# Loading q and k of a windowed attention by GpSimd's casting transfers, with one group of heads worked by token halves and the hand-written order made anew

## The chip, the cores and the metric

The kernel runs on one core of a Trainium2 chip, as one launch. The metric is device time in microseconds (us), the median of several executions. Five engines have queues of their own: PE (TensorE, matrix products), DVE (VectorE), ACT (ScalarE), POOL (GpSimd) and SP (SyncE, which only issues transfers here). A profile of one execution gives the start and the length of every instruction, what it waited for, and the transfers.

## The reference, cut to what matters

```python
B, H, S, D = 8, 8, 576, 64
scores = (1 / sqrt(D)) * q @ k.T                 # per batch and head
mask = (rel >= 0) & (rel < 64)                   # rel = query position - key position
attn = softmax(where(mask, scores, -1e9))
x = (attn @ v) -> [B, S, H * D]                  # 576 tokens x 512

h = relu(x @ w_in)                               # 512 -> 1024
u, v = h[..., :512], h[..., 512:]
v_n = (v - mean(v)) / sqrt(var(v) + 1e-6)        # over the 512 features
v_s = einsum('ts,bsd->btd', w_spatial, v_n) + b_spatial
out = (u * v_s) @ w_out                          # [8, 576, 512], f32
```

All inputs are f32 in memory. The kernel computes in f16 with f32 accumulation.

## The kernel before

The work of a batch falls into steps, each with a name such as `S3_0`: kind S, batch 3, group 0 of the heads (heads 0 to 3; group 1 is heads 4 to 7). The attention steps of a batch and a group are these.

- `ldq`, `ldk`: load q and k of four heads as 128 rows of 1152 numbers. `tq`, `tk` (line 405, DVE): transpose them into `qkT` tiles.
- `ldv`: load V in five chunks of tokens. `hv` holds V in f16, `hs` the same shifted by 64 rows, filled by the copies `sl`, `su` and `s4`.
- `S` (line 494, PE): scores of the band into two pairs of PSUM banks. Step `E` (line 501, ACT): exponential. `M` (line 504, DVE): a minimum with a mask that holds 0 or a large number, which cuts the band. `Z` (line 517, PE): row sums by a matmul with ones. `N` and `n` (lines 544 and 546, ACT): the inverse by Ln and Exp. `P` (line 529, PE): the product with V. `X` (line 537, DVE): the scaling, into the f16 tile `x`. One `E`, `M`, `Z`, `P` and `X` serves two heads with all of the first 512 tokens; the names end in 0 and 1 for the two halves of the group's heads. The last 64 tokens of a batch, or of two batches, go through steps of their own with an `r` in the name (`S0_r`, `X0_r`).

The gating network of a batch has these steps, in 128-token groups `j` or 128-feature groups `i` (4 whole ones and a smaller fifth).

- `V` (x times the second half of w_in, PE), `Vr` (relu, line 684, ACT), `Vb`, `Va` (mean and variance, lines 686 and 688, DVE), `L1`, `L2` (one over the deviation, lines 731 and 733, ACT), `A` (normalise, line 743, DVE).
- `U` (first half of w_in times x, PE), `Ur` (relu, line 778, ACT), `G` (v_n times w_spatial, PE), `Ge` (gating, line 812, DVE), `O` (times w_out, PE), `Oe` (eviction, lines 662 and 850), `st` (store).

A group of V, U or O is four matmuls of 512 columns, a group of G five. The matmuls are issued in `halves` (lines 629 and 632): a step that the order marks `PH` is issued as pairs of 64-column halves. The spatial weights are transposed on PE (`W`, line 361) and copied out (`We`). `D` steps (line 877) are matmuls on zeros whose results nobody reads; they occupy PE at the start.

**Loads.** q and k of batches 0 to 2, V of batches 0 and 1 and all weights come by POOL's queue, whose transfers cast f32 to f16 on the way (lines 330, 344, 384, 422, 436). q and k of batches 3 to 7 come in f32 by SP's queue into eight `nat` buffers (line 395) and are cast by `cq` and `ck` into four `hqk` buffers; on POOL such a cast is three instructions of 384 columns (line 278). V of batches 2 to 7 comes in f32 by SP's queue into four `natv` buffers (line 448) and is cast by `cv`. A one-element copy on POOL, `hold` (line 393), keeps SP's first transfer back until the last early q has landed.

**The order.** The string `ORDER` (lines 18 to 140) lists every step with its engine and the buffers that it takes. `as_listed` (line 178) emits the steps in that order, so each engine and each queue works through its own steps as listed, and waits where something that a step needs isn't there yet. Nothing is reordered at run time.

Of the code, these are the lines that a sentence can't say: the load of q or k, first for batches 0 to 2, then for the others.

```python
c = add(f"ld{name}{b}_{g}", ("POOL", 0.55), key, lambda e: nc.gpsimd.dma_start(
    h.t.bitcast(f16)[:, 0:1152], src[b, 4 * g:4 * g + 4, :, :].rearrange("h (i j) d -> (h i) (j d)", j=18)),
    acq=[h])
...
ld = add(f"ld{name}{b}_{g}", ("DQ", 0.45), key, lambda e: nc.sync.dma_start(
    n.t[:, :], src[b, 4 * g:4 * g + 4, :, :].rearrange("h (i j) d -> (h i) (j d)", j=18)),
    deps=[hold], acq=[] if hold else [n], uses=[n] if hold else [], nbytes=1.57, n=128)
h = buf("hqk", f"h{name}{b}_{g}")
c = add(f"c{name}{b}_{g}", cost(1152), key,
        lambda e: cp(e, h.t[:, :], n.t[:, :]), deps=[ld], acq=[h], uses=[n])
```

Of the kernel before, what the change touches and what calls it, by code (L numbers as in the profile page):

```python
# [18 lines left out]
ldq0_0:POOL:0 ldk0_0:POOL:1 ldk0_1:POOL:2 keep:POOL ldv0_00:POOL:0 D24:PE:0 mask:DVE ldq0_1:POOL:3  # L19
D5:PE:1 ldv0_10:POOL:1 ldv0_01:POOL D21:PE:2 tq0_0:DVE:0 ldk1_0:POOL:4 D18:PE:3 D2:PE:0 D14:PE:1  # L20
D19:PE:2 D10:PE:3 ldv0_14:POOL ldv0_11:POOL D3:PE:0 D1:PE:1 D22:PE:2 D15:PE:3 tk0_0:DVE:1
S0_0:PE:0:1 tk0_1:DVE:2 E0_01:ACT:0 sl0_00:ACT:0 D6:PE:0 D0:PE:1 E0_00:ACT:1 su0_00:ACT D26:PE:2
ldv0_04:POOL M0_01:DVE Z0_01:PE:3 D23:PE:0 D8:PE:1 tq0_1:DVE:3 D16:PE:2 ldq1_0:POOL:5 S0_r:PE:1:0
E0_r0:ACT:0 D7:PE:0 E0_r1:ACT N0_01:ACT:0 M0_00:DVE Z0_00:PE:1 N0_00:ACT:1 ldwin1:POOL M0_r:DVE
Z0_r:PE:2 S0_1:PE:1:0 N0_r:ACT:2 D4:PE:0 sl0_10:ACT:1 tk1_0:DVE:4 su0_10:DVE E0_10:ACT:2 M0_10:DVE
s40_1:DVE sl0_11:DVE D12:PE:3 s40_0:DVE n0_00:ACT D20:PE:1 E0_11:ACT:3 M0_11:DVE sl0_01:POOL
su0_01:POOL P0_00:PE:2 X0_00:DVE:0 D11:PE:0 Z0_10:PE:3 D25:PE:1 su0_11:ACT n0_r:ACT P0_r:PE:0
X0_r:DVE:0 N0_10:ACT:3 n0_10:ACT tq1_0:DVE:5 P0_10:PE:1 Z0_11:PE:3 P0_01:PE:2 N0_11:ACT:4
X0_10:DVE:1 n0_01:ACT X0_01:DVE D13:PE:0 n0_11:ACT S1_0:PE:1:0 E1_00:ACT:1 P0_11:PE:3 E1_01:ACT:2
V0_4:PE:0 Vr0_4:ACT:0 X0_11:DVE V0_0:PH:1 V0_2:PE:2 M1_00:DVE ldq1_1:POOL:6 ldk1_1:POOL:7 M1_01:DVE  # L30
tq1_1:DVE:6 tk1_1:DVE:7 ldwin0:POOL Vr0_0:ACT:1 Z1_01:PE:3 N1_01:ACT:5 V0_1:PH:0 n1_01:ACT
Vr0_1:ACT:2 Vb0_1:DVE:0 V0_3:PH:1 Vr0_3:ACT:3 Vb0_3:DVE:1 Z1_00:PE:3 S1_1:PE:1:0 ldv1_00:POOL:2
Vr0_2:ACT:4 ldwsp0:POOL:0 ldwsp4:POOL:0 Vb0_2:DVE:2 D9:PE:0 ldv1_01:POOL E1_10:ACT:0 U0_4:PE:1
ldq2_0:POOL:1 U0_0:PE:2 U0_3:PE:0 E1_11:ACT:3 S1_r:PE:1:0 Ur0_0:ACT:0 consts:POOL Ur0_3:ACT:1
Vb0_0:DVE:3 Va0_0:DVE Va0_2:DVE M1_10:DVE E1_r0:ACT:0 U0_1:PE:2 ldb:POOL ldk2_0:POOL:2 Vb0_4:DVE:4
Va0_4:DVE sl1_00:DVE:2 Va0_1:DVE E1_r1:ACT Va0_3:DVE M1_11:DVE L10:ACT:0 Ur0_4:ACT:2 ldv1_10:POOL:3
ldv1_11:POOL L20:ACT A0_2:DVE:0 A0_3:DVE:1 A0_4:DVE A0_1:DVE:2 M1_r:DVE Ur0_1:ACT:3 U0_2:PE:0
Ur0_2:ACT:4 N1_00:ACT:1 W2:PE:1 We2:ACT A0_0:DVE:3 W3:PE:2 We3:ACT D17:PE:0 W4:PE:3 We4:ACT
sl1_01:DVE W1:PE:0 W0:PE:1 su1_00:DVE We1:DVE We0:DVE su1_01:DVE Z1_r:PE:2 n1_00:ACT N1_r:ACT:2
Z1_11:PE:0 N1_11:ACT:3 Z1_10:PE:3 G0_4:PH:1 N1_10:ACT:0 tq2_0:DVE:8 P1_00:PE:2 X1_00:DVE:2  # L40
sl1_10:ACT:3 n1_10:ACT su1_10:ACT G0_1:PH:0 ldv1_14:POOL P1_01:PE:3 G0_0:PH:2 Ge0_4:DVE:0
ldv1_04:POOL ldq2_1:POOL:3 tk2_0:DVE:0 X1_01:DVE Ge0_1:DVE:1 G0_2:PH:1 Ge0_2:DVE:2 ldk2_1:POOL:4
ldwo:POOL su1_11:POOL sl1_11:ACT P1_10:PE:3 s41_1:POOL hold:POOL:5 X1_10:DVE:3 S2_0:PE:1:0
P1_11:PE:0 ldq3_0:DQ cq3_0:POOL:0 n1_11:ACT X1_11:DVE s41_0:ACT ldv2_00:DQ:0 ldv2_03:DQ ldk3_0:DQ:6
ldv2_02:DQ G0_3:PH:1 Ge0_3:DVE:3 P1_r:PE:3 ck3_0:POOL:1 ldv2_01:DQ n1_r:ACT E2_01:ACT:1
ldv2_10:DQ:1 ldv2_13:DQ ldv2_14:DQ ldv2_11:DQ X1_r:DVE:1 tq2_1:DVE:1 V1_3:PH:0 E2_00:ACT:2
M2_00:DVE V1_0:PH:1 Vr1_0:ACT:5 tk2_1:DVE:2 V1_1:PH:3 Vr1_1:ACT:6 Ge0_0:DVE:4 Vr1_3:ACT:7 V1_2:PH:1
Vr1_2:ACT:4 V1_4:PE:3 Vb1_2:DVE:5 Vr1_4:ACT:3 M2_01:DVE Va1_2:DVE Vb1_3:DVE:3 Vb1_4:DVE:2
S2_1:PE:0:1 E2_11:ACT:0 U1_4:PE:0 E2_10:ACT:3 Va1_3:DVE U1_2:PE:1 Vb1_1:DVE:4 Va1_4:DVE Ur1_2:ACT:5
O0_2:PE:2 Oe0_4:ACT:0 S2_r:PE:1:0 Oe0_2:ACT:0 E2_r0:ACT:0 E2_r1:ACT Ur1_4:ACT:2 O0_3:PH:1 Oe0_3:ACT  # L50
ldq3_1:DQ:7 Z2_01:PE:3 U1_1:PH:2 N2_01:ACT:4 ldv2_12:DQ M2_11:DVE Va1_1:DVE U1_3:PH:0 Vb1_0:DVE:0
Va1_0:DVE M2_10:DVE L11:ACT:1 Z2_10:PE:1 Ur1_3:ACT:3 L21:ACT N2_10:ACT:1 O0_0:PH:3 U1_0:PH:0
Z2_00:PE:1 Ur1_1:ACT:4 Oe0_0:ACT:1 ldq5_0:DQ:0 tk3_0:DVE:3 tq3_0:DVE:4 S3_0:PE:1:0 Z2_11:PE:2
O0_1:PH:3 Ur1_0:ACT:1 N2_00:ACT:5 N2_11:ACT:0 Oe0_1:ACT M2_r:DVE Z2_r:PE:0 A1_2:DVE:4 A1_0:DVE:5
A1_4:DVE A1_1:DVE:6 A1_3:DVE:7 cv2_10:DVE:0 cv2_00:POOL:1 sl2_00:DVE:0 su2_00:DVE sl2_10:DVE:1
s42_1:POOL ldv2_04:DQ s42_0:POOL su2_10:POOL G1_3:PH:1 Ge1_3:DVE:5 P2_00:PE:2 G1_4:PH:3 ldk4_0:DQ:1
N2_r:ACT:3 n2_r:ACT cq3_1:POOL:2 n2_00:ACT X2_00:DVE:0 Ge1_4:DVE:6 P2_01:PE:0 cq5_0:POOL:3
G1_2:PH:1 n2_01:ACT X2_01:DVE E3_01:ACT:2 n2_11:ACT n2_10:ACT ldk3_1:DQ:2 ck3_1:ACT:1 P2_10:PE:2
M3_01:DVE P2_11:PE:3 ldq4_0:DQ:3 ldk4_1:DQ:4 E3_00:ACT:1 G1_0:PH:0 X2_10:DVE:1 X2_11:DVE
Ge1_0:DVE:7 tq3_1:DVE:5 G1_1:PH:2 Ge1_1:DVE:8 V2_3:PH:3 Vr2_3:ACT:0 V2_1:PH:0 Vr2_1:ACT:2 V2_0:PH:3  # L60
Vr2_0:ACT:1 Z3_01:PE:2 N3_01:ACT:2 V2_2:PH:0 Vr2_2:ACT:4 M3_00:DVE tk3_1:DVE:6 Ge1_2:DVE:9
S3_1:PE:0:1 E3_11:ACT:3 P2_r:PE:3 Vb2_2:DVE:1 cq4_0:POOL:0 st0_1:DQ ck4_0:POOL:2 Z3_00:PE:2
N3_00:ACT:5 E3_10:ACT:0 U2_3:PH:1 st0_4:DQ X2_r:DVE:0 V2_4:PE:0 Vr2_4:ACT:5 Oe1_4:ACT:0 O1_0:PE:3
Oe1_0:ACT:0 ck4_1:POOL:1 Vb2_0:DVE:5 ldv3_10:DQ:2 ldv3_13:DQ ldv3_00:DQ:3 ldv3_01:DQ ldv4_00:DQ:1
ldv4_04:DQ ldv3_11:DQ ldv4_03:DQ ldv3_04:DQ ldv3_12:DQ st0_0:DQ ldv3_14:DQ ldv3_03:DQ st1_4:DQ
ldq4_1:DQ:5 U2_0:PE:2 M3_11:DVE Ur2_0:ACT:0 U2_1:PH:0 Ur2_1:ACT:3 Z3_11:PE:3 tk4_0:DVE:7
Vb2_1:DVE:3 Va2_1:DVE cv3_10:POOL:2 sl3_10:POOL:2 tk4_1:DVE:0 S3_r:PE:1:0 E3_r0:ACT:0 E3_r1:ACT
N3_11:ACT:4 Ur2_3:ACT:2 U2_2:PE:2 Ur2_2:ACT:1 s43_1:POOL Vb2_4:DVE:2 O1_1:PE:0 O1_2:PE:3
cq4_1:POOL:2 Va2_2:DVE O1_3:PE:1 Vb2_3:DVE:4 ldv4_01:DQ Va2_0:DVE tq4_0:DVE:1 S4_0:PE:1:0 Va2_3:DVE
Va2_4:DVE Oe1_1:ACT L12:ACT:0 L22:ACT n3_11:ACT M3_r:DVE M3_10:DVE ldv3_02:DQ ldk5_1:DQ:6  # L70
ldv4_02:DQ su3_10:DVE Z3_r:PE:2 U2_4:PH:0 Oe1_2:ACT:1 Oe1_3:ACT N3_r:ACT:1 Ur2_4:ACT:4 Z3_10:PE:3
P3_10:PE:1 N3_10:ACT:0 n3_r:ACT n3_10:ACT P3_11:PE:2 A2_3:DVE:0 A2_1:DVE:1 A2_2:DVE:2 A2_0:DVE:3
A2_4:DVE G2_0:PE:0 E4_01:ACT:0 G2_2:PE:3 tq4_1:DVE:2 cv3_00:DVE:3 sl3_00:POOL:3 Ge2_0:DVE:0
X3_10:DVE:2 X3_11:DVE E4_00:ACT:3 s43_0:DVE Ge2_2:DVE:1 su3_00:ACT G2_4:PE:0 n3_00:ACT n3_01:ACT
G2_3:PE:1 Ge2_4:DVE:2 S4_1:PE:0:1 cv4_00:POOL:1 Ge2_3:DVE:3 P3_r:PE:2 P3_00:PE:3 X3_r:DVE:1
X3_00:DVE:3 G2_1:PE:0 P3_01:PE:1 V3_4:PE:2 E4_11:ACT:1 E4_10:ACT:2 M4_00:DVE X3_01:DVE Oe2_4:ACT:0
Ge2_1:DVE:4 Vr3_4:ACT:3 M4_11:DVE sl4_00:POOL:0 su4_00:POOL Z4_00:PE:3 N4_00:ACT:3 ldk5_0:DQ:7
ck5_0:POOL:1 V3_3:PH:1 Vr3_3:ACT:6 V3_1:PH:0 Vr3_1:ACT:7 n4_00:ACT V3_2:PH:2 Vr3_2:ACT:0 M4_01:DVE
Vb3_3:DVE:0 M4_10:DVE ldv5_00:DQ:0 V3_0:PH:3 Vr3_0:ACT:2 ldv5_10:DQ:2 ldv5_14:DQ ldv5_12:DQ
ldq6_1:DQ:2 ldv4_10:DQ:3 st1_0:DQ tq5_0:DVE:8 Vb3_4:DVE:3 Va3_4:DVE Z4_01:PE:1 Z4_11:PE:0  # L80
N4_01:ACT:0 n4_01:ACT N4_11:ACT:4 U3_1:PH:2 U3_0:PH:3 Ur3_1:ACT:5 Ur3_0:ACT:0 O2_0:PH:1 Vb3_2:DVE:1
cq6_1:POOL:0 Vb3_1:DVE:5 ldv4_12:DQ ldv5_04:DQ ldq5_1:DQ:0 ldv5_13:DQ cq5_1:POOL:2 ck5_1:POOL:3
Z4_10:PE:0 N4_10:ACT:1 P4_00:PE:2 Vb3_0:DVE:4 Va3_2:DVE X4_00:DVE:0 Va3_3:DVE Va3_0:DVE s44_0:ACT
Va3_1:DVE L13:ACT:1 Oe2_0:ACT:0 U3_3:PH:3 st1_1:DQ Ur3_3:ACT:1 tk5_0:DVE:3 ldq6_0:DQ:3 L23:ACT
tk5_1:DVE:4 A3_2:DVE:4 A3_4:DVE A3_0:DVE:5 U3_4:PE:0 U3_2:PE:2 Ur3_2:ACT:4 O2_2:PE:1 S5_0:PE:1:0
Ur3_4:ACT:2 A3_1:DVE:6 P4_01:PE:3 X4_01:DVE A3_3:DVE:7 E5_01:ACT:3 tq5_1:DVE:5 ldv4_11:DQ
ldv5_11:DQ ldv4_14:DQ M5_01:DVE ldv4_13:DQ ldk7_1:DQ:1 ldv5_02:DQ O2_1:PH:2 Oe2_1:ACT Oe2_2:ACT:1
O2_3:PH:0 Oe2_3:ACT E5_00:ACT:0 G3_3:PH:3 Ge3_3:DVE:6 M5_00:DVE G3_1:PH:2 Ge3_1:DVE:5 cv4_10:POOL:0
st2_4:DQ Z5_01:PE:1 sl4_10:POOL:1 s44_1:POOL G3_2:PH:0 G3_0:PH:3 su4_10:POOL P4_10:PE:2 ldv5_01:DQ
ldv5_03:DQ cv5_00:ACT:2 n4_10:ACT Ge3_2:DVE:7 N5_01:ACT:5 n4_11:ACT sl5_00:DVE:2 su5_00:POOL  # L90
# [842 lines left out]
```

## Time and profile before

| | us |
|---|---|
| median of 3 runs | 195.82 (195.31 to 196.53) |
| the profiled execution | 195.76 |
| its span, first to last instruction | 194.1 |
| PE busy | 185.5 |
| DVE busy | 162.0 |
| ACT busy | 150.5 |
| POOL busy | 84.7 |

How to read the rows that follow. A row of the timeline has the start in us from the span's start, the length, the engine, the line of the code, the operation, and what it writes and reads; in brackets stand the idle time of the engine just before it and what ended that. PEld are weight loads, which overlap the matmuls. A row of the groups has the busy time and the mean in nanoseconds of one instruction. POOLq and SPq are the queues' own entries. Of a matmul the end is modelled, so that lengths of matmuls overlap; the spacing of their starts tells the pace.

### The profile page before, as it was taken

The numbers are of one execution on the slowest core, as the hardware profiler recorded it, in microseconds if no ns is written. First come the engines' busy times: TensorE is split into PE (matmuls) and PEld (weight loads), VectorE is DVE, ScalarE is ACT, GpSimd is POOL, SyncE is SP. The second block draws the span as 40 slices with busy tenths as digits, with TensorE's granted clock in tenths as the row PEclk, the third lists the DMA queues.
The fourth block names the chain that finished last, engine by engine and source line by source line (L and its number), as shares of the span: only waits on it lengthen the run. The fifth ranks groups of instructions, "written<-read, shape, count | busy, mean of one in ns | idle before, by whom it ended". The sixth has DMA issues, their size and how long they took to land.

```text
span 194.1 us, 7423 instructions
## 1 busy us (share of the span) xinstructions
PE 185.5 (96%) x3167; PEld 112.0 (58%) x3167; DVE 162.0 (83%) x310; ACT 150.5 (78%) x272; POOL 84.7 (44%) x151
## 2 busy tenths in 40 slices
...
GB/s 72 190 164 187 197 193 181 143 225 301 208 351 396 223 184 220 322 277 264 269 232 243 328 320 148 84 257 179 5 75 77 111 5 0 138 0 137 132 140 191
DMA packets 50257, 35.74 MB, mean 184 GB/s; under 512 B 39216, under 2 KB 41712, under 8 KB 50224
## 3 DMA queue, kind: packets, MB, share of 16 engines
...
q8 instruction: 24, 0.39, 0.8%
...
## 4 chain that ended last, share of the span: by engine, by line
PE 74%; DMA 10%; POOL 6%; DVE 5%; issue 3%; DVEq 0%; POOLq 0%
PE bank L632 46%; PE bank L629 13%; DMA wsp<-in_moe_w_spatial_dram 6%; PE bank L529 4%; PE pair L494 4%; PE bank L517 3%; DMA hq<-in_q_dram 3%; POOL hv L422 3%; PE bank L717 3%; DMA hv<-in_v_dram 1%; POOL hk L384 1%; DVE x L537 1%; PE bank L612 1%; POOL hq L384 1%; PE bank L720 1%
## 5 line engine op out<-in xcount | busy, mean ns | idle before, releaser
L501 ACT ACTIVATE e<-pair 128x1024 f16<-128x1024 f32 x32 | 32.0, 1026 | 9.7 <-PE pair L494 8.4
L632 PE MATMUL bank<-wspT,vn 128*64 128x512 f16 (+3 forms) x460 | 34.9, 299 | 0.3 <-DVE x L537 0.2
L662 ACT COPY ob<-bank 128x512 f32<-128x512 f32 (+1 forms) x38 | 22.0, 591 | 11.9 <-PE bank L632 8.0
L686 DVE BATCH_NORM_STATS2 st<-vs 128x6 f32<-128x512 f16 (+1 forms) x40 | 26.2, 672 | 5.6 <-ACT vs L684 5.5
L812 DVE TENSOR_TENSOR g<-bank,ru 128x512 f16<-128x512 f32 (+1 forms) x36 | 23.0, 653 | 8.0 <-PE bank L632 5.3
L684 ACT ACTIVATE vs<-bank 128x512 f16<-128x512 f32 (+1 forms) x40 | 22.9, 595 | 7.0 <-PE bank L632 5.3
L632 PE MATMUL bank<-win,x 128*64 128x512 f16 x224 | 28.0, 380 | 0.0
L632 PEld LDWEIGHTS <-vn 128*64 128x64 f16 (+1 forms) x460 | 19.5, 111 | 11.6 <-issue 0.7
L632 PE MATMUL bank<-wout,g 128*64 128x512 f16 (+1 forms) x208 | 24.9, 371 | 0.0
L778 ACT ACTIVATE ru<-bank 128x512 f32<-128x512 f32 (+1 forms) x38 | 21.5, 581 | 4.0 <-PE bank L629 2.0
L632 PE MATMUL bank<-x,win 128*64 128x512 f16 (+2 forms) x264 | 24.1, 318 | 0.0
L504 DVE TENSOR_TENSOR e<-e,mask 128x1024 f16<-128x1024 f16 x32 | 22.3, 701 | 1.0 <-ACT e L501 0.9
L278 POOL CAST hq<-nq 128x384 f16<-128x384 f32 x24 | 13.2, 589 | 21.1 <-DMA nq<-in_q_dram 21.1
L537 DVE TENSOR_TENSOR x<-bank,lz 128x512 f16<-128x512 f32 x32 | 21.4, 681 | 1.1 <-PE bank L529 0.3
L405 DVE STREAM_TRANSPOSE kT<-hk 128x576 f32<-128x576 f32 x16 | 19.7, 1242 | 1.6 <-DMA hk<-in_k_dram 1.6
L544 ACT ACTIVATE lz<-bank 128x512 f32<-128x512 f32 x32 | 18.8, 598 | 2.6 <-PE bank L517 2.5
L405 DVE STREAM_TRANSPOSE qT<-hq 128x576 f32<-128x576 f32 x16 | 19.9, 1244 | 0.2
L546 ACT ACTIVATE lz<-lz 128x512 f32<-128x512 f32 x32 | 19.8, 631 | 0.3
L632 PEld LDWEIGHTS <-x 128*64 128x64 f16 x224 | 14.6, 110 | 8.6 <-issue 0.3
L278 POOL CAST hk<-nk 128x384 f16<-128x384 f32 x27 | 14.7, 579 | 8.6 <-DVE st L686 2.7
L632 PEld LDWEIGHTS <-g 128*64 128x64 f16 x208 | 13.8, 110 | 6.7 <-issue 0.4
L632 PEld LDWEIGHTS <-win 128*64 128x64 f16 x264 | 13.1, 110 | 7.2 <-issue 0.9
...
## 6 DMA issues: line engine op xcount, KB each, us to landing
...
hq<-in_q_dram POOLq DMA_DIRECT2D x6, 288.0 KB, 5.4
hk<-in_k_dram POOLq DMA_DIRECT2D x6, 288.0 KB, 6.1
...
```

Of the source, the lines that this page charges most:

```text
L278: nc.gpsimd.tensor_copy(o[:, n:n + 384], i[:, n:n + 384])
L405: d = add(f"t{name}{b}_{g}", ("DVE", 1.09), key, lambda e: nc.vector.transpose(qt.t[:, :].rearrange("p (i j) -> p j i", j=18), (h.t[:, 0:5 ...
L501: ex = add(f"E{b}_{g}{u}", ("ACT", 0.91), key, lambda e, u=u: nc.scalar.activation(e2[u].t[:, :, :], sc[u].t[:, :, :], AF.Exp, bias=0.0, s ...
L504: mins.append(add(f"M{b}_{g}{u}", ("DVE", 0.65), key, lambda e, u=u: nc.vector.tensor_tensor(e2[u].t[:, :, :], e2[u].t[:, :, :], mask[:, : ...
L537: lambda e, u=u, ob=ob, lz=lz: nc.vector.tensor_tensor(x.t[:, u, :], ob.t[:, :], lz.t[:, :], ALU.mult),
L629: nc.tensor.matmul(o[:, :], w, x, start=start, stop=stop)
L632: nc.tensor.matmul(o[c:c + 64, :], w[:, c:c + 64], x, start=start, stop=stop)
L662: lambda e: (nc.vector.tensor_copy if last else nc.scalar.copy)(view(), m.t[rows, 0:n]),
L684: rl = add(f"Vr{b}_{j}", ("ACT", 0.49), key, lambda e: nc.scalar.activation(vs.t[0:jn, :], m.t[0:jn, :], AF.Relu), deps=[pv], acq=[vs], us ...
L686: s1 = add(f"Vb{b}_{j}", ("DVE", 0.6), key + 0.02, lambda e: nc.vector.bn_stats(st6.t[0:jn, 0:6], vs.t[0:jn, :]), deps=[rl], acq=[st6], us ...
L778: lambda e, m=m, ru=ru, n=n: nc.scalar.activation(ru.t[:, 0:n], m.t[:, 0:n], AF.Relu), deps=[pu], acq=[ru], uses=[m])))
L812: nc.vector.tensor_tensor(g.t[:, 0:n], m.t[:, 0:n], ru.t[:, 0:n], ALU.mult)
```

## The change

- q and k of all batches are loaded by POOL's casting transfers, straight into `hqk`, of which there are now twelve. The steps `cq` and `ck` of batches 3 to 7 are gone, and the `nat` buffers too. The spatial weights pass through a `natv` buffer.
- V of batches 2 to 7 stays on SP's queue in f32, with six `natv` buffers instead of four. `hold` now waits for the last early V load and stands on POOL before the first V transfer of SP.
- Group 1 of batch 0 is worked by token halves: a new function `by_token` has one E (in two instructions), M, Z, N, n, P and X for 256 tokens of all four heads instead of 512 tokens of two heads. V0_0 and V0_1 need the first half only, V0_2 and V0_3 both heads' second half.
- The filler is 11 steps of four matmuls with 256 columns and 28 steps of one with 512, where it was 25 steps of two with 512 and two of nine with 128.
- The whole order is new. At its start the k and q loads of both groups of batch 0 come first on POOL, then `consts`, V loads, and `keep`; the mask stands on DVE behind the fourth transpose. All filler stands ahead of the first V0 step. In the new order one `cv` runs on ACT and one on DVE, ten on POOL (before: two, three and seven). The last output group is O7_5, evicted on ACT.

```diff
+BYTOKEN = {(0, 1)}
-NWARM, NFILL, FILL = 27, 2, 9
-BUFS = {"nat": 8, "natv": 4, "hqk": 4, ...
+NWARM, NFILL, FILL = 39, 28, 1
+BUFS = {"natv": 6, "hqk": 12, ...
...
-            if b <= 2:
-                h = buf("nat", f"h{name}{b}_{g}")
...
             h = buf("hqk", f"h{name}{b}_{g}")
-            c = add(f"c{name}{b}_{g}", cost(1152), key,
-                    lambda e: cp(e, h.t[:, :], n.t[:, :]), deps=[ld], acq=[h], uses=[n])
+            c = add(f"ld{name}{b}_{g}", ("POOL", 0.55), key, lambda e: nc.gpsimd.dma_start(
+                h.t[:, :], src[b, 4 * g:4 * g + 4, :, :].rearrange("h (i j) d -> (h i) (j d)", j=18)),
+                acq=[h])
...
+            if (b, g) == (2, 0):
+                held = HELD[0]
+                lds.append(add("hold", [("POOL", 0.1), ("ACT", 0.1)], key, lambda e: cp(
+                    e, nv.t[0:1, 0, 0, 0:1], held.t[0:1, 4, 0, 0:1]), deps=[HELD[1]], acq=[nv], uses=[held]))
...
+    def by_token(b, g, key, s, sc, e2):
...
+        for t in (0, 1):
+            ts = slice(256 * t, 256 * t + 256)
+            et = e2[t]
...
+                    lambda e, u=u, et=et, ts=ts: nc.scalar.activation(
+                        et.t[:, u, :].rearrange("p (w q) -> p w q", w=2), sc[u].t[:, :, ts],
+                        AF.Exp, bias=0.0, scale=0.125),
...
+                    for u in (0, 1):
+                        for w in (0, 1):
+                            nc.tensor.matmul(zb.t[64 * w:64 * w + 64, 256 * u:256 * u + 256], ones[:, :],
+                                             et.t[:, u, 256 * w:256 * w + 256], start=True, stop=True)
...
-                     deps=[XD[b, r] for r in range(4)] + [WIN[1, r] for r in range(4)],
+                     deps=[XD[b, r] for r in range(4)
+                           if not ((b, r // 2) in BYTOKEN and j // 2 != r % 2)]
+                     + [WIN[1, r] for r in range(4)],
...
-            for c in range(2 if i < NWARM - NFILL else FILL):
-                n = 512 if i < NWARM - NFILL else 128
+            for c in range(4 if i < NWARM - NFILL else FILL):
+                n = 256 if i < NWARM - NFILL else 512
```

The new order at the places that matter below (step, engine, buffer):

```diff
+ldk0_0:POOL:0 tk0_0:DVE:0 D0:PE:0 D1:PE:1 D2:PE:2 D3:PE:3 ldq0_0:POOL:1 tq0_0:DVE:1 D4:PE:0 D5:PE:1
+D6:PE:2 D7:PE:3 ldk0_1:POOL:2 ldq0_1:POOL:3 consts:POOL ldv0_00:POOL:0 ldv0_04:POOL ldv0_01:POOL
+keep:POOL ldk1_0:POOL:4 D8:PE:0 S0_0:PE:0:1 E0_00:ACT:0 E0_01:ACT:1 tk0_1:DVE:2 tq0_1:DVE:3 D9:PE:1
+D10:PE:2 D11:PE:3 D12:PE:0 ldv0_10:POOL:1 ldq1_0:POOL:5 ldv0_14:POOL D13:PE:1 D14:PE:2 D15:PE:3
+D16:PE:0 D17:PE:1 S0_r:PE:0:1 E0_r0:ACT:0 mask:DVE M0_00:DVE sl0_00:DVE:0 sl0_01:DVE E0_r1:ACT
+su0_01:DVE M0_01:DVE D18:PE:2 D19:PE:3 M0_r:DVE D20:PE:0 D21:PE:1 ldv0_11:POOL ldwin1:POOL D22:PE:2
+S0_1:PE:0:1 ldk1_1:POOL:6 E0_11a:ACT:2 E0_10a:ACT:3 ldq1_1:POOL:7 D23:PE:3 ldwin0:POOL su0_00:ACT
...
+D24:PE:0 ... Z0_00:PE:3 N0_00:ACT:0 tk1_0:DVE:4 E0_10b:ACT ... M0_10:DVE ...
+M0_11:DVE ... tq1_0:DVE:5 sl0_10:DVE:1 ... X0_00:DVE:0 su0_11:DVE su0_10:DVE ...
+s40_1:DVE s40_0:DVE ... X0_01:DVE D38:PE:1 n0_11:ACT X0_10:DVE:1 X0_11:DVE ...
+V0_1:PH:1 V0_3:PE:2 Z1_01:PE:3 ... V0_2:PH:0 ... V0_4:PE:2 ... Z1_00:PE:1 ... V0_0:PH:0 ... S1_1:PE:1:0
...
+s42_1:POOL ... ldk3_1:POOL:3 ldq4_0:POOL:4 ... ldk4_1:POOL:5
...
+su4_00:POOL tq4_1:DVE:2 ... ldq5_1:POOL:11
...
+st7_40:DQ Oe7_3:ACT st7_3:DQ st7_41:ACT O7_1:PH:3 Oe7_1:ACT O7_5:PH:2 Oe7_5:ACT st7_5:ACT st7_1:DQ
```

313 lines of the change are left out of this document (169 added, 144 removed).

## The prediction, made before the changed kernel ran

> **What bounds the kernel now.** I read the page's busy table first, then the same sums by stage (busy time of each engine between two times), then the chain of waits.
>
> ```profile
> span 194.1 us, 7423 instructions
> ...
> PE 185.5 (96%) x3167; PEld 112.0 (58%) x3167; DVE 162.0 (83%) x310; ACT 150.5 (78%) x272; POOL 84.7 (44%) x151
> ```
> ```profile
> 21.70:36.20 14.50, 14.26 (x192) 7.39 (x188) 13.64 (x30) 13.58 (x27) 9.99 (x17) 1.00 1.45 174
> ...
> 43.00:190.00 147.00, 145.84 (x2476) 89.98 (x2470) 126.20 (x240) 117.97 (x215) 54.75 (x97) 1.00 0.65 189
> ```
> ```profile
> 18.41 11.90 DMA wsp<-in_moe_w_spatial_dram
> ...
> 109.59 0.55 issue
> ...
> 112.54 5.18 PE bank L632 x48
> ```
> The columns of the second fence are: length of the stretch, then busy time of PE, weight loads, DVE, ACT and POOL, granted clock, DMA share, GB/s. From 43.0 to 190.0 PE is busy 145.84 of 147.00 us, at a clock of 1.00: this long stretch is bound by TensorE, and the change takes no matmul of the computation away. In it 24 pairs of half-width matmuls take 5.18 us, 0.216 us a pair, so a group V, U or O of four pairs costs 0.86 us and a group G of five 1.08. What is left to win there is idle time: 147.00 - 145.84 = 1.16 us, of which the chain names one piece of 0.55 at 109.59. Busy time of PE near the start says little, since most of it there is filler of line 877. So two stretches can move the end: the start, until PE has dense work, and the last 4 us. DVE is the engine behind both start stretches: from 21.7 to 36.2 it is busy 13.64 of 14.50.
>
> **The start, now.** These are DVE's instructions, of the timeline (start, length, what):
>
> ```profile
> 3.86 0.18 DVE L306 COPY mask<-keep 128x64 f16<-128x64 f16 x1 [2.52 <-POOL keep L302]
> ...
> 5.58 1.25 DVE L405 STREAM_TRANSPOSE qT<-hq 128x576 f32<-128x576 f32 x1
> 6.99 1.26 DVE L405 STREAM_TRANSPOSE kT<-hk 128x576 f32<-128x576 f32 x1 [0.16 <-DMA hk<-in_k_dram]
> 8.69 1.26 DVE L405 STREAM_TRANSPOSE kT<-hk 128x576 f32<-128x576 f32 x1 [0.45 <-DMA hk<-in_k_dram]
> ...
> 10.92 1.26 DVE L405 STREAM_TRANSPOSE qT<-hq 128x576 f32<-128x576 f32 x1
> 12.02 0.68 DVE L504 TENSOR_TENSOR e<-e,mask 128x1024 f16<-128x1024 f16 x1
> 13.62 0.43 DVE L589 TENSOR_TENSOR er<-er,mask 128x512 f16<-128x512 f16 x1 [0.93 <-ACT er L578]
> ...
> 17.33 0.69 DVE L283 COPY hs<-hv 64x256 f16<-64x256 f16 x3
> ...
> 20.69 2.04 DVE L537 TENSOR_TENSOR x<-bank,lz 128x512 f16<-128x512 f32 x3
> ```
> and these PE's, where the spatial-weight groups G0 and the second batch's V1 begin:
>
> ```profile
> 23.59 0.39 PE L629 MATMUL bank<-win,x 128*128 128x512 f16 x1
> ...
> 35.27 0.30 PE L597 MATMUL bank<-er,ones 128*64 128x128 f16 x4
> 35.74 0.62 PE L517 MATMUL bank<-e,ones 128*64 128x512 f16 x4 [0.17 <-DVE wspT L283]
> 36.17 0.82 PE L632 MATMUL bank<-wspT,vn 128*64 128x64 f16 x40
> ...
> 43.00 0.39 PE L632 MATMUL bank<-win,x 128*64 128x512 f16 x2
> ```
> By 23.59, where the third V0 group begins, two are done (1.7 us), so dense work began in effect near 21.9. I use 43.00, the first V1, as the mark: what lies before it is the start.
>
> **The start, after.** The first four transfers on the POOL queue are now k, q, k, q of batch 0, without V between. Successive loads were taken up at 5.58, 6.99 and 8.69, so 1.41 and 1.70 us apart; the fourth should be there at 10.1 to 10.4, I take 10.2, against 10.92 now. Against that, the mask, hidden on DVE from 3.86 to 5.58 until now (1.72 us), moves behind the fourth transpose, because `keep` stands behind `consts` and five V transfers in POOL's order. It now lies on DVE's own path. DVE's list up to X0_10, the piece that frees V0_1: transpose 1.26, mask 1.72, M0_00 0.68, three copies 0.7, M0_01 0.68, M0_r 0.43, a transpose 1.26, M0_10 and M0_11 1.36, a transpose 1.26, one copy 0.23, X0_00 0.68, four copies 0.92, X0_01 and X0_10 1.36: 12.5 us, from 10.2 to 22.7. Successive DVE instructions overlap a little (10.92 + 1.26 is 12.18, yet the next starts at 12.02); at up to 0.1 for some ten of them the end is 21.7 to 22.7, I take 22.2. The token halves show here: V0_1 starts without X0_11, the last quarter, which adds 0.68. Other costs of the halves: four exponentials of half size in place of two whole ones on ACT, and four Z matmuls in place of two of twice the width, the same columns. Both lie beside the DVE list.
>
> From 22.2 PE has five V0 groups 4.3, two Z 0.43, S1_1 0.6, four U0 groups 3.46, U0_4 0.47, S1_r 0.23 and the five W transposes 2.3 (estimates: 0.216 a pair, and for S, Z and W the pace of their steps in this trace): 34.0. The filler D9 and D17, which stood among them, is now ahead of V0. The other road to G0 is DVE again:
>
> ```profile
> L686 DVE BATCH_NORM_STATS2 st<-vs 128x6 f32<-128x512 f16 x32 | 21.1, 675 | 1.7 <-ACT vs L684 1.6
> ...
> L743 DVE TENSOR_SCALAR vn<-vs,mv,ln 128x512 f16<-128x512 f16 x32 | 12.7, 436 | 1.6 <-ACT ln L733 1.5
> ...
> L733 ACT ACTIVATE ln<-ln 128x5 f32<-128x5 f32 x8 | 1.6, 205 | 0.2
> ```
> X0_11 0.68, two masks 1.36, X0_r 0.4, two transposes 2.5, five statistics 3.4, a mask 0.68, five aggregates 0.5, Ln and Exp on ACT 0.5, five normalisations 2.2, two wspT copies 0.8, less the same overlap of 1.0: 22.2 + 12.0 = 34.2. So G0 starts near 34.4. Now it starts at 36.17 with three Z steps done before it (35.27 to 36.17, about 0.5 of real work), so at 35.6 on equal terms: 1.2 us gained. The spatial weights, 11.90 us in the chain now, land about as before or 0.8 earlier (one V pair no longer stands ahead of them), so they do not decide. From G0 to V1 the work is the same. **Start: -1.2 us**, with bounds -2.2 (overlap full, fourth load at 10.1) and +0.5 (no overlap, fourth load as late as now).
>
> **The middle.** What goes and what comes:
>
> ```profile
> L278 POOL CAST hk<-nk 128x384 f16<-128x384 f32 x27 | 14.7, 579 | 8.6 <-DVE st L686 2.7 <-DVE x L537 2.3 <-DVE qT L405 1.8
> L278 POOL CAST hq<-nq 128x384 f16<-128x384 f32 x24 | 13.2, 589 | 21.1 <-DMA nq<-in_q_dram 21.1
> L275 ACT CAST hq<-nq 128x1152 f16<-128x1152 f32 x1 | 1.2, 1152 | 0.0
> L283 DVE CAST hq<-nq 128x1152 f16<-128x1152 f32 x1 | 0.7, 744 | 0.0
> L283 DVE CAST hv<-nv 128x1024 f16<-128x1024 f32 x3 | 2.0, 680 | 0.0
> ```
> ```profile
> L384 POOL DMA_DIRECT2D hq<-in_q_dram x6: 543/572/666, 1.3 to 34.0; - x6
> L278 POOL CAST hq<-nq x24: 497/502/1096, 46.1 to 133.8; 128x384 f16<-128x384 f32 x24
> ```
> Twenty casts go: 27.9 us on POOL, 0.7 on DVE, two of about 1.15 on ACT. In the new order one V cast stays on DVE instead of three (-1.4) and one on ACT instead of two (-1.0). Some copies move too, three away from DVE (-0.7). Twenty issues come to POOL, 20 x 0.57 = 11.4 us, and leave SP. POOL was 54.75 of 147 busy, so this is hidden under PE. DVE loses some 2.8 of 126.2 us and ACT 3 to 4 of 118. PE waits for these two in the middle, so I take two thirds of the 1.16 idle: **-0.8 us**, bounds +1.5 (the new order brings a few waits of its own, each like the 0.55) and -1.2, all idle gone; waits shorter than a matmul's own 0.38 us do not show as idle, so -2 is not excluded.
>
> [...]
>
> **The tail.** Now and after, the last eviction and its store set the end:
>
> ```profile
> 187.54 0.38 ACT L850 COPY ob<-bank 128x256 f32<-128x256 f32 x1
> 189.18 0.59 ACT L662 COPY ob<-bank 128x512 f32<-128x512 f32 x1 [0.28 <-PE bank L632]
> 189.41 0.61 PE L861 MATMUL bank<-wout,g 128*64 128x256 f16 x8
> 190.11 0.42 DVE L662 COPY ob<-bank 128x256 f32<-128x256 f32 x1
> ```
> Now 0.70 us pass from 189.41 to the last copy and 0.42 in it. After, O7_5 (0.43) comes last, its 0.38 copy stands on ACT behind O7_1's 0.59 copy. Counted from the last group's start that is 0.2 + 0.48 + 0.38 = 1.06 against 1.12: **-0.05**.
>
> **Sum.** -1.2 - 0.8 - 0.05 = -2.05. The profiled execution took 195.76 us around its 194.1 us span, 0.06 under the median of 195.82: 195.76 - 2.05 = **193.7 us**.
>
> **Rivals.** First, *the start gives nothing*: the mask on DVE's path eats the earlier q, the G0 mark stays at 35.6, and only the middle's 0.8 and some of a new wait's 0.55 remain: about 195.3. For it: 1.72 us of mask against 0.7 of earlier q. Second, *the middle gives more*: PE's short waits for DVE and ACT go as well, -2 there, 192.5, or 191.5 with a start at its good bound. For it: DVE is nearly full until about 110; against: idle is 1.16. Third, *slower: loads behind copies on POOL.* The q and k loads now stand in POOL's order with the V casts and copies, which wait for V:
>
> ```profile
> POOL hv L281 <- DMA nv<-in_v_dram: 7.0, 4, 4.5
> POOL hs L283 <- DMA nv<-in_v_dram: 5.2, 1, 5.2
> ```
> ```profile
> hq<-in_q_dram POOLq DMA_DIRECT2D x6, 288.0 KB, 5.4
> ```
> ldk3_1, ldq4_0 and ldk4_1 stand behind s42_1, ldq5_1 behind su4_00. Between ldq5_1 and its transpose stand nine PE groups, about 8 us. With a wait of 5.2, a landing of 5.4 and the transpose of 1.26 a load is 3.9 us late, and PE stands: 193.7 + 3.9 = 197.6. It decides when POOL reaches a load less than 6.7 us before its transpose's turn. Against: twelve buffers let POOL run ahead by two batches. [...]
>
> **Chances.** Forecast 0.45 (own range 192.6 to 194.8), start gives nothing 0.22, middle gives more 0.18, slower 0.15. A measurement here tells about 1% from no change, so faster means under 193.9. The forecast case lies under it for 0.28 of its 0.45; with the second rival faster is 0.46; same is 0.17 + 0.22 = 0.39; slower 0.15. The range runs from the second rival's 191.5 to 197.2, which takes in the start's and the middle's bad bounds together but for 0.6 (195.76 + 0.5 + 1.5 = 197.8) and leaves out the worse half of the third.
>
> **What would show it.** Right: V0's first group near 22.2, G0's first near 34.4, V1's first near 41.8; issues of q and k on POOL near 0.57 us; no cast of nq or nk; PE idle from V1 on below 1 us. Wrong: the mask ends after 13.7, a q or k transpose of batches 3 to 7 waits for its DMA, or POOL's issues are 1 us and more.

## The result and the profile after

| | before | after |
|---|---|---|
| median, us | 195.83 (195.31 to 196.53, 4 runs) | 198.84 (198.28 to 202.82, 4 runs) |
| the profiled execution, us | 195.76 | 199.15 |
| its span, us | 194.1 | 197.2 |
| PE, DVE, ACT, POOL busy, us | 185.5, 162.0, 150.5, 84.7 | 184.8, 159.4, 148.8, 77.7 |

The kernel became slower: the ratio of after to before is 1.0119, with a 95% interval of 1.0075 to 1.0163. (The execution of 202.82, at a mean clock of 0.981, is left out of the ratio.) The forecast was 193.7, its range ended at 197.2.

I read the profile after as I had read that of before, the long stretch first. These are the busy times by stretch, with the columns of the prediction (length, PE, weight loads, DVE, ACT, POOL, clock, DMA share, GB/s):

```profile
84.00:98.00 14.00, 13.94 (x251) 8.60 (x248) 13.36 (x26) 12.29 (x24) 10.54 (x18) 1.00 0.99 222
98.00:113.50 15.50, 14.10 (x260) 7.82 (x258) 11.25 (x19) 13.35 (x24) 2.77 (x5) 1.00 0.98 182
...
43.30:193.00 149.70, 144.81 (x2490) 87.93 (x2484) 123.92 (x233) 118.01 (x216) 45.70 (x76) 1.00 0.65 150
```

From the first V1 group to 193.0, PE is idle for 149.70 - 144.81 = 4.89 us; before it was 1.16. PE's timeline shows one place that makes most of it:

```profile
111.25 1.03 PE L685 MATMUL bank<-wout,g 128*64 128x512 f16 x8
115.90 0.62 PE L513 MATMUL bank<-e,ones 128*64 128x512 f16 x4 [3.62 <-DVE e L500]
```

The two Z steps of batch 5's second heads wait for a mask step of DVE. So DVE's timeline comes next:

```profile
109.20 0.29 DVE L282 CAST hs<-nv 64x256 f16<-64x256 f32 x1
113.54 0.69 DVE L282 CAST hv<-nv 128x1024 f16<-128x1024 f32 x1 [4.06 <-DMA nv<-in_v_dram]
114.15 0.68 DVE L642 TENSOR_TENSOR er<-er,mask 128x1024 f16<-128x1024 f16 x1
114.75 1.09 DVE L500 TENSOR_TENSOR e<-e,mask 128x1024 f16<-128x1024 f16 x1
```

The masks were not late by themselves. DVE stood 4.06 us in `cv5_10`, the cast of batch 5's second V, and `M5_r` and `M5_11` are behind it in DVE's list. What was late is V. The timelines of the two that issue transfers, SP and POOL:

```profile
98.04 0.38 SPq L730 DMA_DIRECT2D out_dram<-ob  x1
98.47 12.58 SPq L441 DMA_DIRECT2D nv<-in_v_dram  x9
```
```profile
95.89 1.40 POOL L280 CAST hv<-nv 128x512 f16<-128x512 f32 x2 [1.51 <-PE bank L682]
97.36 1.23 POOL L280 COPY hs<-hv 64x512 f16<-64x512 f16 x2
98.54 1.17 POOL L386 DMA_DIRECT2D hq<-in_q_dram  x2
99.69 1.08 POOL L386 DMA_DIRECT2D hk<-in_k_dram  x2
```

From 98.47 on SP issues nine pieces of V, the first of them (`ldv5_11`) needed by `cv5_10`, the last three of that V (`ldv5_14`, `_13`, `_12`) at places 6 to 8. At 98.54 to 100.2 POOL issues four casting loads, which had stood behind POOL's cast and copies of V and so leave together. The view of the transfers, cut to 102 to 108 us, shows what the DMA engines did then (packets, MB, share of the 16 engines; q0 is POOL's queue, q1 SP's), and the same view for the issues from 98.4 to 102.6 shows how long V took (KB each, median us to landing):

```profile
q0 software_dynamic: 506, 1.04, 92.8%
q1 hardware_dynamic: 500, 0.13, 15.0%
```
```profile
hq<-in_q_dram POOLq DMA_DIRECT2D x2, 288.0 KB, 6.5
hk<-in_k_dram POOLq DMA_DIRECT2D x2, 288.0 KB, 9.0
...
nv<-in_v_dram SPq DMA_DIRECT2D x3, 128.0 KB, 10.9
nv<-in_v_dram SPq DMA_DIRECT2D x2, 64.0 KB, 10.6
```

In these 6 us the two queues sent about as many packets, 500 and 506. SP's are nearly all rows of V; of POOL's, 1.04 MB makes some 450 rows of q or k, and the rest are writes of 4 B (the view counts 553 packets under 512 B, so 53 of POOL's). But a row of V has 256 B and one of q 2304 B, and POOL's packets held the engines for 92.8% of the time: by these shares some 0.20 us for a row of q and 0.03 for one of V. From 108 to 110, with POOL's four loads nearly through (31 packets), SP's queue moved 1709. A piece of V took 10.9 us where the median of all of SP's V loads is 4.8. And the DMA engines were full anyway: their share is 0.98 and 0.99 in the two stretches above.

Two theories for the stall, then. **A, the order**: SP's list issues the last pieces of this V behind four pieces of later batches. **B, the shared engines**: q and k have a queue of their own now and hold up V whatever SP's order is.

For the start, the marks are these rows of PE:

```profile
22.63 1.05 PE L685 MATMUL bank<-win,x 128*64 128x512 f16 x8
...
35.22 1.25 PE L682 MATMUL bank<-wspT,vn 128*128 128x512 f16 x5
...
43.30 1.04 PE L682 MATMUL bank<-win,x 128*128 128x512 f16 x4
```

V1's first group is at 43.30 in place of 43.00: the start gave nothing. **Theory C**: the mask, which now stands on DVE's path, ate the gain.

### The profile page after: what moved, and what is told of

Read it like the earlier page. It is cut to its first block, busy times and chain, and to the rows that moved or that the text cites. A ratio compares the mean times of both kernels' runs of the same rounds, so it can differ in the third digit from the quotient of the medians.

```text
span 197.2 us, 7410 instructions
## 1 busy us (share of the span) xinstructions
PE 184.8 (94%) x3188; PEld 111.2 (56%) x3188; DVE 159.4 (81%) x304; ACT 148.8 (75%) x271; POOL 77.7 (39%) x134
## 4 chain that ended last, share of the span: by engine, by line
PE 55%; DVE 22%; DMA 6%; ACT 5%; issue 5%; SPq 4%; POOL 1%; DVEq 0%; POOLq 0%
PE bank L685 35%; PE bank L682 7%; SPq L441 4%; DMA hq<-in_q_dram 4%; DVE e L500 3%; PE bank L772 3%; PE pair L487 3%; DVE st L739 3%; DVE kT L393 3%; DMA nv<-in_v_dram 2%; PE bank L525 2%; DVE g L867 2%; PE bank L513 2%; DVE x L533 2%; DVE qT L393 2%
## 5 line engine op out<-in xcount | busy, mean ns | idle before, releaser
L685 PE MATMUL bank<-wspT,vn 128*64 128x512 f16 (+3 forms) x550 | 41.8, 299 | 0.0
L497 ACT ACTIVATE e<-pair 128x1024 f16<-128x1024 f32 x30 | 29.8, 1021 | 9.1 <-PE pair L487 8.7
L280 POOL COPY hs<-hv 64x512 f16<-64x512 f16 (+1 forms) x36 | 22.7, 661 | 21.4 <-DVE hv L282 13.6
L685 PEld LDWEIGHTS <-vn 128*64 128x64 f16 (+1 forms) x550 | 23.1, 111 | 13.1 <-DVE vn L798 0.5
L280 POOL CAST hv<-nv 128x512 f16<-128x512 f32 x20 | 13.0, 671 | 38.1 <-DMA nv<-in_v_dram 21.2
L685 PE MATMUL bank<-win,x 128*64 128x512 f16 x216 | 26.7, 379 | 0.0
L685 PE MATMUL bank<-x,win 128*64 128x512 f16 (+1 forms) x216 | 21.8, 332 | 0.0
L533 DVE TENSOR_TENSOR x<-bank,lz 128x512 f16<-128x512 f32 x30 | 20.0, 681 | 0.7 <-PE bank L525 0.2
L798 DVE TENSOR_SCALAR vn<-vs,mv,ln 128x512 f16<-128x512 f16 (+1 forms) x40 | 15.5, 442 | 4.2 <-ACT ln L788 4.2
L685 PEld LDWEIGHTS <-g 128*64 128x64 f16 x200 | 12.1, 110 | 7.0 <-issue 0.3
```

Source lines behind the costliest of these rows:

```text
L280: nc.gpsimd.tensor_copy(o[:, lo:hi, :, :], i[:, lo:hi, :, :])
L497: ex = add(f"E{b}_{g}{u}", ("ACT", 0.91), key, lambda e, u=u: nc.scalar.activation(e2[u].t[:, :, :], sc[u].t[:, :, :], AF.Exp, bias=0.0, s ...
L533: lambda e, u=u, ob=ob, lz=lz: nc.vector.tensor_tensor(x.t[:, u, :], ob.t[:, :], lz.t[:, :], ALU.mult),
L685: nc.tensor.matmul(o[c:c + 64, :], w[:, c:c + 64], x, start=start, stop=stop)
```

## The experiments

**V of batch 5 first on SP.** Ratios here and below are to the kernel before, on the same chip. The kernel after was not run again there, so its own ratio, 1.0119, is what they stand against.

```diff
-ldv4_04:DQ ldv6_00:DQ:3 ldv7_10:DQ:4 ldv7_14:DQ ... ldv5_14:DQ ldv5_13:DQ ldv5_12:DQ s45_0:DVE cv5_10:DVE:3
+ldv5_14:DQ ldv5_13:DQ ldv5_12:DQ ldv4_04:DQ ldv6_00:DQ:3 ldv7_10:DQ:4 ldv7_14:DQ ... s45_0:DVE cv5_10:DVE:3
```

> The last three pieces of batch 5's second V (ldv5_14, ldv5_13, ldv5_12) are issued on SP's queue ahead of four pieces of batches 4, 6 and 7; nothing else moves. Theory A (the order on SP's queue): these pieces went out at 106.47 to 108.69, behind four others; now they go out by 101.5, land with the usual 5 us at about 106, the cast cv5_10 starts at its turn on DVE (109.5 against 113.54), the idle of PE of 3.62 us at 112 is gone and the time is 199.15 - 3.6 = 195.5. Theory B (the DMA engines are shared between two queues, and the four casting loads of q and k that POOL issues from 98.5 to 100.2 starve the small rows of V): the piece ahead of them, ldv5_11, went out at 98.47 already and landed at 110.53 only; it will land there again, the three behind it at 110.9 to 111.9, the cast starts near 111.9 and half the stall, 1.6 to 2.0 us, is left: about 197.4.

Measured: 194.87 us (193.06 to 198.21, 10 runs), ratio 0.990 (0.9855 to 0.9946). The stall is gone, PE is busy 13.00 of the 13 us from 98 to 111. That is A's number, but the trace shows more than A. Here the issues of V from 97.7 to 101.3, and, in a second fence, those from 101.8 to 103.5, just after POOL's first casting load at 101.83:

```profile
L441 SPq DMA_DIRECT2D nv<-in_v_dram x5: 505/607/1505, 97.8 to 101.2; - x5
...
DMA to landing us min/median/max: 2.7/2.8/4.0
```
```profile
L441 SPq DMA_DIRECT2D nv<-in_v_dram x3: 461/550/607, 101.9 to 103.1; - x3
...
DMA to landing us min/median/max: 6.1/10.3/10.4
```

V that went out before the casting loads took 2.8 us, V that went out after them 10.3. The repair moved the right pieces ahead of the casting loads, by 0.6 us. B's mechanism is there; its forecast failed because POOL came 3.3 us later here than in the profile after.

**Three casting loads behind V.**

```diff
-... Oe2_1:ACT ldq7_0:POOL:3 Z5_11:PE:2 ... ldk7_1:POOL:4 ldk6_1:POOL:5 ... sl5_10:POOL:3
+... Oe2_1:ACT sl5_10:POOL:3 ldq7_0:POOL:3 Z5_11:PE:2 ... ldk7_1:POOL:4 ldk6_1:POOL:5 ...
```

> POOL's copy sl5_10, which needs all of batch 5's second V, is put ahead of the three casting loads ldq7_0, ldk7_1 and ldk6_1, so these are issued only when that V has landed; SP's list is as before. Theory A (order on SP's queue): the last pieces still go out near 108.7 and land at 113, the stall stays, 199. Theory B (the casting loads starve V): with one casting load in place of four beside it, ldv5_11 lands by 105 in place of 110.53, SP's issues are no longer held up (one of them took 3.96 us), all four pieces are there by 108, the 3.62 us of idle are gone and the time is near 195.5, unless ldk6_1 now comes too late for its transpose.

Measured: 194.67 us (193.6 to 195.73), ratio 0.9904 (0.9859 to 0.995). SP's list is that of the kernel after, piece for piece, and the stall is gone. All eight pieces from 98.3 on:

```profile
L441 SPq DMA_DIRECT2D nv<-in_v_dram x8: 451/606/1140, 98.3 to 103.4; - x8
...
DMA to landing us min/median/max: 3.0/3.6/4.5
```

So A alone is refuted: the order on SP does no harm when the casting loads stay away. With the run before, either thing that parts the two takes the stall away.

**The cast of V on POOL.**

```diff
-... s45_0:DVE cv5_10:DVE:3 Ur4_0:ACT:3 ... sl5_10:POOL:3
+... s45_0:DVE Ur4_0:ACT:3 ... cv5_10:POOL:3 sl5_10:POOL:3
```

> The cast cv5_10 goes from DVE to POOL, just ahead of sl5_10; the order of all transfers is the same. Both theories leave the landing of V at 113.0 to 113.5. If the stall is made by DVE's order (the masks M5_r and M5_11 stand behind the waiting cast, Z5_11 and Z5_10 wait for the masks), these four run at once and PE goes on; POOL then needs two casts of 0.61, two copies of 0.6 and 0.4 and two of 0.61 after 113.5, so P5_10 finds its V at 117.2 where PE would be at 115.6: 1.6 us of idle at another place, total about 197.1. If the masks wait for something else, no change: 199.

Measured: 194.61 us (193.67 to 195.5), ratio 0.9913 (0.9874 to 0.9953). POOL's cast starts at 113.21 after 8.96 us of waiting for V, so V is as late as in the kernel after, and yet most of the stall is gone. What is left stands where expected, in two pieces of 0.88 and 0.24 us and short waits, about 1.5 in all:

```profile
115.55 0.22 PE L525 MATMUL bank<-e,hs 128*64 128x64 f16 x2 [0.88 <-POOL hs L280]
...
116.11 0.22 PE L525 MATMUL bank<-e,hs 128*64 128x64 f16 x2 [0.24 <-POOL hs L280]
```

That shows the last link: a late V cost 3.62 us because DVE, in order, held two masks behind it that had no need of V. The total fell 2.5 us further than the 197.1 that I expected; this was not traced in full.

**The loads alone.** This run and the next are one execution each. In the first the stages overlapped, so that its numbers are bounds only: V alone landed in 3.0 to 3.3 us, beside casting loads in 9.4 to 11.2.

> Loads alone, six stages one after the other, each of four pieces of V (128 KB, rows of 256 B) or four loads of q (128 rows) or both; nothing of the reference is computed, the output is zeros. From the kernel after: a casting row holds its DMA engine 218 ns, an f32 row 223 ns, a V row 20 ns; so four loads of q are 7 us of all 16 engines and four pieces of V 2.5 us. Stage a, V on SP alone: last piece lands 2.5 to 3.5 us after its issue. Stage b, four casting loads alone: the last lands about 7 us after the first begins to move. Stage c, four casting loads on POOL and V on SP issued at the same time. Theory B (rows of both queues take turns, each turn of q ten times as long): V lands with or after the last of q, 8 to 10 us after its issue. Theory A (the queues share by bytes or not at all): V lands within 5 us. Stage d, q as f32 and V behind it, both on SP: V lands after q, about 8 us. Stage e, q as f32 on ACT's queue and V on SP: as c if any two queues do it, within 5 us if it is a matter of the casting queue. Stage f, all on POOL, q first: as d.

The second run parts the stages by copies on DVE.

```diff
+    phases = [("a", nc.gpsimd, 0, 1), ("b", nc.gpsimd, 4, 0), ("c", nc.gpsimd, 1, 1), ("d", nc.gpsimd, 2, 1),
+              ("e", nc.gpsimd, 4, 1), ("f", nc.scalar, 4, 1), ("g", nc.sync, 4, 1), ("h", nc.sync, 4, 0),
+              ("i", nc.gpsimd, 4, 2)]       # queue of q, loads of q, V (2: ahead of q)
```

> The loads alone again, with stages that do not overlap: nothing of the reference is computed. In each stage four pieces of V (128 KB, rows of 256 B) go out on SP's queue, beside none, one, two or four casting loads of q on POOL issued at the same moment (stages a, c, d, e), beside four f32 loads of q on ACT's queue (f), behind four f32 loads on SP's own queue (g), and 1 us or more ahead of four casting loads (i); stage b is four casting loads alone, h four f32 loads alone. If rows of the two queues take turns and a row of q holds its engine ten times as long as one of V, the last V piece lands with the last load of q: about 3 us after its issue alone, then 5, 7 and 10 as one, two and four casting loads stand beside it, 8 to 10 in f as well, and 3 to 4 in i, where V has gone ahead. If it is a matter of the casting queue alone, f stays at 4. Casting buys no DMA time: b and h take the same from first to last landing, 1.5 to 1.8 us a load.

Measured, in the view of the transfers (median to landing of four pieces of V; the last letter is the stage):

```profile
va<-in_v_dram SPq DMA_DIRECT2D x4, 128.0 KB, 2.9
vc<-in_v_dram SPq DMA_DIRECT2D x4, 128.0 KB, 4.7
vd<-in_v_dram SPq DMA_DIRECT2D x4, 128.0 KB, 4.9
ve<-in_v_dram SPq DMA_DIRECT2D x4, 128.0 KB, 7.1
vf<-in_v_dram SPq DMA_DIRECT2D x4, 128.0 KB, 8.5
vg<-in_v_dram SPq DMA_DIRECT2D x4, 128.0 KB, 7.4
vi<-in_v_dram SPq DMA_DIRECT2D x4, 128.0 KB, 3.3
```

The slowest piece took 3.0 us alone (a), 4.9, 5.7 and 9.2 beside one, two and four casting loads (c, d, e). It is not a matter of casting: with q as f32 on ACT's queue (f) it was 8.6. Behind q on SP's own queue (g) it was 7.5: there V waits too, but a list for one queue says so. In stage i three pieces went ahead and took 2.2 to 3.7 us; the fourth was issued at 72.49, 0.3 us after the first casting load, and landed at 82.4.

The last rows of that piece went out beside rows of q. The view of the transfers from 81.5 to 82.0 gives the rate in 40 slices of 0.0125 us, and the packets of the two queues:

```profile
GB/s 0 205 0 184 0 0 0 0 0 0 0 0 0 0 0 184 0 20 0 184 0 0 0 0 0 0 0 0 0 0 0 0 0 20 0 0 0 0 0 0
...
q0 software_dynamic: 7, 0.01, 10.2%
q1 hardware_dynamic: 4, 0.00, 1.3%
```

In one slice a row of V is 20 GB/s, a row of q 184, and one of each 205. So a row of V started at 81.52, 81.72 and 81.92, 0.20 us apart, and a row of q takes 0.19 us in this trace (from 78.0 to 82.4 q0's 301 packets, 40 of them small, held the 16 engines for 72.4% of the time). It was much the same since 78.0: the view from there to 82.4 has 23 packets of q1, the piece's last 22 rows and one small write, and the rows came some 0.18 us apart. Each load or piece has 16 such small writes here (stage b: 576 packets for four loads of 128 rows; stage e: 2112 of q1 for four pieces of 512), so 15 of this one's were out before 78.0. That only one of the 16 engines was left with the 22 rows is my estimate from this; no view names the engine of a packet. The last row started at 81.92, the sixteenth write is the fourth packet of q1 above, and the piece was reported landed at 82.4.

The spacing fits queues that take turns row by row: one row of V in 0.20 us, beside a row of q of 0.19 us.

Casting bought no time of the DMA engines here: four casting loads alone (b) held them for 79.9% of 8.3 us, 6.6 us, four f32 loads (h) for 73.2% of 8.6, 6.3 us.

**The casting loads alone in the old order.** From the kernel before: q and k of batches 3 to 7 on POOL at the places that SP had, the casts gone, 16 `hqk` buffers and a fifth `natv` for the spatial weights.

```diff
-ldq3_0:DQ cq3_0:POOL:0 ... ldk3_0:DQ:6 ... ck3_0:POOL:1
+ldq3_0:POOL:12 ... ldk3_0:POOL:13 ...
```

> The kernel before with the first part of the change alone: q and k of batches 3 to 7 come by casting loads on POOL at the places in the list where SP had them, the twenty casts are gone (27.9 us of POOL's work), and everything else, the order, the mask, the halves by heads, is as before. Theory A (the new order made the stall, the queues are innocent): no slower than before, 194.5 to 195.8. Theory B (what makes V late is that q and k now have a queue of their own beside it): V pieces issued beside casting loads take 10 us and more here too, where the list was made for one queue; 197 to 200, with PE waiting for V or for a copy that waits for V.

Measured: 200.65 us, ratio 1.0233 (1.0164 to 1.0302). That looked like B, but two filler steps had come out too long, and V1 stood at 46.92. So once more, with the filler of the kernel before:

> As the kernel before with casting loads of q and k alone, but with the filler matmuls of the kernel before too: in the earlier run two filler steps had come out with 512 columns in place of 128 (2.99 against 1.54 us and 1.90 against 0.68), and V1's first group stood at 46.92 in place of 43.00 because of it, while from there to the last group 145.92 us passed against 145.97. If only the filler made that run slow: V1 near 43.0 to 44.0 and 195.5 to 197.0, which means that casting loads in the old order cost nothing by themselves and bring nothing, though POOL is freed of 27.9 us (Theory A). If sharing the DMA engines between two queues costs in this order too (Theory B), PE waits for V or its copies somewhere from V1 on: 198 and more.

Measured: 195.99 us (194.89 to 197.86, 10 runs), ratio 0.999 (0.9958 to 1.0023). By itself the first part of the change is worth nothing, though it takes 27.9 us of casts off POOL (whose busy time falls from 84.7 to 66.7). The profiled execution is a long one, 197.72 us, and it shows that the loads are not simply harmless. SP, in its timeline:

```profile
87.42 12.88 SPq L443 DMA_DIRECT2D nv<-in_v_dram  x5
```

Five casting loads had gone out from 85.7 to 87.8; V's pieces of that time took up to 14.3 us to land, one issue on SP took 7.92 us, and PE waited for V's copies with 0.99 and 0.25 us near 106. Behind these waits the granted clock fell to 0.50, from 107.5 to 110.9. So B's mechanism works in the old order too, at another place and with a smaller stall. How often it does, and what it is set off against in the executions near the median, I did not separate.

**The mask early.**

```diff
-ldk0_0:POOL:0 tk0_0:DVE:0 ... consts:POOL ldv0_00:POOL:0 ldv0_04:POOL ldv0_01:POOL keep:POOL ... mask:DVE M0_00:DVE
+ldk0_0:POOL:0 ldq0_0:POOL:1 ldk0_1:POOL:2 ldq0_1:POOL:3 keep:POOL mask:DVE tk0_0:DVE:0 ... consts:POOL ... M0_00:DVE
```

> The small mask source (keep) is built on POOL right after the first four loads, ahead of the constants and of V, and the mask itself is made on DVE ahead of its first transpose, so the mask leaves DVE's path behind the fourth transpose. Theory C (the mask of 1.72 us cost the start its gain): V0's first group goes from 22.63 to 21.0, G0's first from 35.22 to 33.6, V1's first from 43.30 to 41.7. Rival (ACT's list is next: the exponential E0_11b ends at 17.10 and the masks M0_10 and M0_11 need it): only 0.6 us come, V0 at 22.0. Of the total, either may lose its part again in the stall at 112, if that stall is set by the time at which V lands: between 197.5 and 199.2.

Measured: 198.78 us (196.73 to 199.8, 4 runs), ratio 1.0141 (1.0036 to 1.0246). V0's first group is at 22.50, G0's at 35.09, V1's at 43.29, where theory C had 21.0, 33.6 and 41.7. Five profiled kernels have one and the same start: the kernel after, each repair of the stall, both together, and the cast on POOL. Their V0 is at 21.95 to 22.63 and their V1 at 42.70 to 43.84. So 0.1 us can't be told here, but 1.6 can, and theory C falls. DVE's timeline of this run has no mask behind the fourth transpose, and waits in its place:

```profile
13.09 1.19 DVE L282 COPY hs<-hv 64x512 f16<-64x512 f16 x2 [0.95 <-DMA hv<-in_v_dram]
...
16.98 1.29 DVE L557 TENSOR_TENSOR e<-e,mask 128x1024 f16<-128x1024 f16 x2 [0.47 <-ACT e L549]
```

`keep` now stands ahead of V on POOL, whose first load of V goes out at 5.85 instead of 5.14, and DVE waits for V; and the exponentials of the second heads come no sooner than ACT's list lets them. The mask had filled gaps that were there anyway.

**Halves by heads again.**

```diff
-BYTOKEN = {(0, 1)}
+BYTOKEN = {}
-E0_11a:ACT:2 E0_10a:ACT:3 ... E0_10b:ACT ... E0_11b:ACT
+E0_11:ACT:2 E0_10:ACT:3 ...
```

> Batch 0's second heads go back to halves by heads (two whole exponentials in place of four of half size, V0's first group then needs both halves of x); loads, mask and order stay. If the token halves are worth what the prediction said (the last quarter of x, 0.68 us, no longer stands ahead of V0's first group): V0's first group at 23.3 in place of 22.63, G0's first at 35.7 to 35.9, V1's first at 43.8 to 44.0. Rival (ACT's two whole exponentials end earlier than four halves and give it back): V0 within 0.2 of 22.63. The stall at 112 stays in both, total 198.5 to 199.8.

Measured: 201.11 us (200.72 to 202.03, 4 runs), ratio 1.0236 (1.018 to 1.0293). V0 is at 22.68 (after: 22.63) and V1 at 43.64. Both lie within 0.1 us of what the five kernels with that start and token halves reach (21.95 to 22.63, and 42.70 to 43.84). So no worth of the token halves shows; but the 0.68 that I gave them is as wide as that spread, and one profile can't rule it out. The total is worse than that of the kernel after by the two ratios (1.0236 and 1.0119, some 2.3 us), for another reason, which stands in the stretches around the stall:

```profile
110.00:113.90 3.90, 1.36 (x14) 0.47 (x10) 1.14 (x2) 1.63 (x3) 0.28 (x1) 1.00 0.86 207
113.90:121.60 7.70, 6.47 (x112) 3.62 (x114) 5.51 (x8) 4.64 (x8) 5.12 (x9) 0.56 0.95 220
121.60:194.00 72.40, 72.25 (x1176) 46.15 (x1170) 54.28 (x113) 49.52 (x92) 8.91 (x14) 1.00 0.27 85
```

PE stood 3.77 us here, from 111.36 to 115.13, and the granted clock, 0.56 in the mean of the 7.7 us from 113.9 on, cost some 3 us of work (an estimate: 0.44 of the 6.47 us in which PE was busy there). In the profile after PE stood 3.62 us and the clock stayed at 1.00.

**Both repairs.**

The diffs of the first two experiments together.

> The last V pieces of batch 5 first on SP (as in the first experiment) and three casting loads behind sl5_10 on POOL (as in the second), the rest of the change whole. Each alone took the stall away; together they should not add up, 194.3 to 194.9, but the cast cv5_10 should be free of the race between the two queues in every execution, so no execution near 198 is left. If the two repairs hurt each other (three loads late for their transposes): above 195.5.

Measured: 194.39 us (194.29 to 194.93, 6 runs), ratio 0.9894 (0.9851 to 0.9936): faster than the kernel before, and by the two ratios than the kernel after. The two don't add up. None of the six executions is near 198, where with V first alone two of ten had been; those two were not profiled, so that the stall was in them is not shown. From V1 on:

```profile
42.70:188.00 145.30, 144.58 (x2489) 87.69 (x2484) 123.20 (x233) 117.72 (x216) 44.87 (x76) 1.00 0.66 154
98.00:113.00 15.00, 15.00 (x332) 8.86 (x330) 14.50 (x22) 13.95 (x26) 6.97 (x12) 1.00 0.73 151
```

PE is idle for 0.72 us of 145.30, where it was 1.16 of 147.00 before.

**Both repairs and the mask early.** The diffs of the mask and of both repairs together.

> The kernel with both repairs of the stall, and the mask built early on top. With the stall gone, what the start gives must show in the total. Theory C (the mask of 1.72 us on DVE's path is what the start lacks): 194.4 - 1.2 = 193.2. Rival, from the run with the mask early alone (V0 at 22.50 against 22.63, DVE now waiting 0.95 for a V piece that comes later and 0.47 for ACT): 194.2 to 194.5, no difference to be measured from the kernel with both repairs.

Measured: 194.79 us (194.23 to 196.2, 11 runs), ratio 0.9931 (0.9901 to 0.9962). No gain: the rival holds, now in the total as well. The profiled execution, the longest of the eleven, names a further line that stands close behind DVE at the start, the transfer of w_in:

```profile
22.94 0.41 PE L685 MATMUL bank<-win,x 128*64 128x512 f16 x2 [0.24 <-DMA win<-in_moe_w_in_dram]
```

## Why the prediction was wrong

**The middle, -0.8, was the step that failed**, by 3.5 us: from V1 to 4 us before the end 149.70 us passed instead of 147.00, so +2.7, with 4.89 us of idle instead of 1.16. The prediction measured the middle by PE's 1.16 us of idle, set POOL's issues and casts against POOL's free time, and bounded the loss by "a few waits of its own, each like the 0.55". The transfers themselves had no term. Yet the row that I had quoted for 43.0 to 190.0 carries a DMA share of 0.65, and that is a mean over a full and an empty part. In the kernel before the share by stage is

```profile
43.00:59.00 16.00, 15.97 (x286) 9.46 (x282) 15.81 (x31) 13.83 (x28) 6.40 (x12) 1.00 1.00 297
...
98.00:113.50 15.50, 14.95 (x328) 8.87 (x328) 14.31 (x25) 12.49 (x22) 8.94 (x15) 1.00 1.01 282
113.50:130.00 16.50, 16.47 (x314) 10.44 (x312) 14.80 (x29) 15.69 (x31) 8.19 (x15) 1.00 0.68 177
```

Until about 113 the DMA engines were as full as PE (a share of 0.93 to 1.01 in each of the five stages). The change moved twenty loads to another queue, and who went first then depended on queue and order: V of the same stage took 3.6 us with three casting loads held back (the second experiment) and 10.9 us beside all four in the kernel after.

**The third rival** had the right sign and the wrong victim. It made q and k late, behind POOL's copies of V, and that its 197.6 lies nearest to the measured 198.84 is luck. The runs showed the reverse: the loads that had gathered behind those copies left together and made V late, on the other queue, and DVE's order carried that to PE.

**The start, -1.2**, gave nothing, as the first rival had it, but not for the rival's reason. The fourth transpose started at 10.53 (I took 10.2) and V0 at 22.63 (22.2): DVE's list was sized nearly right. But it is one of several lines of about the same length, as the early mask showed: V's landing, ACT's exponentials and w_in's transfer stand just behind it. G0 came at 35.22 (34.4), and from there to V1 8.08 us passed. The work was the same, as I had said: these matmuls, three Z steps among them, took the 7.73 us from 35.27 on before. So at G0 the start was ahead by 0.05 us and not by 1.2, and it lost 0.35 behind it. PE counts as busy for 8.02 us there, against 7.56, which fits waits too short to show as idle.

**Right** were the price of an issue on POOL (1.17 and 1.08 us for two, at 98.54 and 99.69, with DVE busy for 2.36 of the 2.50 us from 98.5 to 101.0; the median of all 32 is 0.55), the tail (its last copy ends 3.6 us before the span's end, as before), and, once the stall is out, the direction of the middle. The size was not: in the profile of both repairs 145.86 us pass from V1 to the last copy, 147.53 before, so -1.7, near the second rival's -2. That the total, 194.39 against 196.71 before on that chip, comes near the forecast's -2.05 is luck: a middle that gave more made up for a start that gave little (V1 at 42.70 instead of 41.8).
